# Regrouping attention heads so that two pairs share their loads

## The chip, the cores and the metric

The kernel runs on one core of a Trainium2 chip. The core has five engines that this document speaks of: PE (TensorE, matmuls and transposes through the PE array), DVE (VectorE), ACT (ScalarE), POOL (GpSimd) and SP (SyncE, which here only issues transfers). Each engine takes its instructions strictly in its own order and stops at an instruction whose semaphore has not come. The metric is the device time of one execution in microseconds (us).

## The reference

Three layers follow one another: attention with a decay, a mixture of experts with one expert per token, and a gated feed-forward layer. The change touches only the first:

```python
# q, k, v: (4, 8, 576, 64), f: (4, 8, 576)
scores = scale * np.matmul(q, k.transpose(0, 1, 3, 2))
cum = np.cumsum(np.log(np.clip(f, 0.0001, 1.0)), axis=-1)
decay = cum[:, :, :, None] - cum[:, :, None, :]
scores = np.where(causal, -1000000000.0, scores + decay)
scores = scores - np.max(scores, axis=-1, keepdims=True)
attn = np.exp(scores)
attn = attn / (np.sum(attn, axis=-1, keepdims=True) + 1e-09)
attn_out = np.matmul(attn, v)
# then x = attn_out as (4 * 576, 512) -> moe(x) -> gated layer(x)
```

In every row of scores the term of the query's own `cum` is constant and drops out of the softmax, so the kernel only needs the key's `cum` ("the sums"), the same for all queries of a head.

## The kernel before, in words

**Stages.** Attention takes the first 222.6 us of the span, then comes a short tail in which the last tokens are routed and scattered to their experts (to 240.4 us), then the experts and the gated layer (to the end). The change leaves the code of the last two alone, except for the order of three weight loads.

**Pairs.** Attention works on 16 pairs of heads, four pairs to each of the four batches; pair p of a batch is heads 2p and 2p + 1. The 576 queries of a head are cut in five chunks: chunks 0 to 3 of 128 queries, and a last one of 64. The last 64 queries of both heads of a pair are stacked, head 0 on partitions 0 to 63 and head 1 on partitions 64 to 127; this chunk is called 4. A pair goes through its chunks from 4 down to 0, and causality makes chunk c read only the keys up to its own.

**Steps of a pair.** SP loads queries and keys (`load_qk`, L344, eight transfers of 72 KB in runs of 128 bytes), V (`load_v`, L336, two of 128 KB and one of 32 KB), the sums of both heads copied to all 128 partitions, keys 0 to 511 (`load_bc`, L356, 512 KB), and for chunk 4 a second copy of the sums, all 576 keys, in which partitions 0 to 63 hold head 0 and 64 to 127 hold head 1 (`load_dec`, L363, two of 144 KB). DVE transposes queries and keys (L402). POOL spreads the last queries (`qk_z`, L446), adds the causal mask of the last 64 keys to the second copy (`dec_m`, L454), and masks the diagonal block of every chunk and head in the common copy (`bc_m`, L459, eight per pair, chunk 3 first). PE makes the scores (L469 for chunk 4, the first of a pair; L481 for the others), DVE adds the sums and takes each row's extreme in one pass (L495; L505 for chunk 4, in two halves of 288 keys over all 128 partitions), ACT takes the exponentials (L513), PE transposes the result (L528) and DVE or ACT bring it to SBUF (L541, L539), and PE multiplies by V (L581). After each batch POOL multiplies the tokens by their route and scatters them (L729, L737), in between the pairs of the next batch. `zero_rows` (L620) clears the place of the scattered tokens by one transfer of 640 KB.

**What sets the order.** The order of every engine is fixed when the kernel is built. A planner (`Plan`, L59) list-schedules about 100 tasks for each pair with assumed durations and priorities. A task's priority is its pair number plus an offset from the table `PR`; a task can only be planned when its inputs and its buffers (`NB`, L269) are there by the planner's own times. On the chip each engine keeps that order whatever the real times are. So a `dec_m` whose transfer lands later than was planned holds every mask that stands behind it on POOL, and by these masks DVE and PE.

**Buffers.** Two tiles for queries and two for keys (one pair each), three for the common copy of the sums, three for the second copy, four for V, two for scores in PSUM.

```python
o.bc = two.tile([P, 2, 512], F32, tag="bc", name="bc", bufs=NB["bc"])
nc.sync.dma_start(out=o.bc, in_=cum_d[None, h : h + 2, :512].to_broadcast([P, 2, 512]))
d = pairs[p].dec[:, 512:576]
nc.gpsimd.tensor_tensor(out=d, in0=d, in1=future, op=ALU.add)
```

Of the kernel before, what the change touches and what calls it, by code (L numbers as in the profile page):

```python
# [24 lines left out]
    ldd=-0.906,  # L25
    ldq=-2.409,
    ldk=-2.46,
    bc=-1.878,
    ldv=-1.485,
    tq=-3.414,  # L30
    tk=-2.813,
    z=-3.857,
    dc=4.332,
    sc=0.044,
    mx=-0.165,
    ex=0.003,
    tr=0.413,
    ev=0.272,
    mk=-0.849,
    rsc=2.696,  # L40
    av=0.888,
    ave=-2.088,
    tok=1.048,
    toe=-2.57,
    rt=1.92,
    rm=0.004,
    rw=2.342,
    step=0.149,
    zr=0.627,
    stick=0.371,  # L50
    w=1.575,
    ws=-0.918,
# [105 lines left out]
def moe_kernel(ctx: ExitStack, tc: tile.TileContext, q, k, v, f, wgate, w1, w2, m2g, m2v, m2o, out):  # L158
# [78 lines left out]

    sel = one.tile([P, NP, 2, W2], F32, name="sel")
# [7 lines left out]
    v_sb = pairwise("v_sb", [P, NC, 2, D], 4)  # L246
# [109 lines left out]
    def load_bc(p):  # L356
        b, hp = divmod(p, NP)
        o = pairs[p]
        o.bc = two.tile([P, 2, 512], F32, tag="bc", name="bc", bufs=NB["bc"])
        h = b * H + 2 * hp  # L360
        nc.sync.dma_start(out=o.bc, in_=cum_d[None, h : h + 2, :512].to_broadcast([P, 2, 512]))

    def load_dec(p):  # L363

        b, hp = divmod(p, NP)
        o = pairs[p]
        o.dec = two.tile([P, S], F32, tag="dec", name="dec", bufs=NB["dec"])
        h = b * H + 2 * hp
        for x in range(2):
            nc.sync.dma_start(  # L370
                out=o.dec[x * 64 : x * 64 + 64], in_=cum_d[None, h + x, :].to_broadcast([64, S])
            )

    def bc_mm(hh, x, st):

        if hh == 2:
# [4 lines left out]
        st.n = 288 if hh == 2 else 256
        st.ps = s_tile()[:, 0]

        for h, a, m in ((0, 0, 64), (1, 64, 64)) if hh == 2 else ((hh, 0, P),):
            nc.tensor.matmul(
                st.ps[a : a + m, : st.n], lhsT=ident[: B * H, h : h + 1].to_broadcast([B * H, m]),
                rhs=setup[1][:, x * st.n : x * st.n + st.n], start=True, stop=True,
            )

    def bc_ev(hh, x, st):  # L390
        o = pairs[0]
        d = o.dec if hh == 2 else o.bc[:, hh]
        nc.scalar.activation(out=d[:, x * st.n : x * st.n + st.n], in_=st.ps[:, : st.n], func=AF.Copy)
# [4 lines left out]
    def qk_t(p, i):  # L398
# [3 lines left out]
        nc.vector.transpose(out=o.t[:, i], in_=o.qk[i][:, :S])  # L402
# [1190 lines left out]
```

## Time and profile before

| | us |
|---|---|
| median of 3 runs (924.0 to 925.56) | 924.26 |
| the profiled execution | 927.53 |
| its span | 925.3 |
| attention, from the span's start | 222.6 |
| routing and scatter of the last tokens | 222.6 to 240.4 |
| experts and gated layer | 240.4 to 925.3 |

The profiled execution is 3.27 us above the median, 2.23 us of it outside the span. Over the span PE is busy 96%, DVE 63%, ACT 43% and POOL 29%. PE's share is lower and the transfers' share higher in the first quarter, where attention is.

In the rows below, a row of the stage table has the stretch, its length, and then for each engine the busy us with the number of instructions, the granted TensorE clock (1.00 is full speed), the share of the DMA engines' time that was in use, and GB/s. A row of a timeline has the start, the duration, the engine, the line, the operation, output and inputs, and in brackets the idle time just before it with what ended it. A row of the waits has the waiting engine and line, who it waited for, the total in us, how often, and the longest. A row by line and shape has the engine, operation and shape with its count, then the busy time and the mean in ns of one, then the idle time before the group with what ended it.

### The profile page before, as it was taken

How to read it: one execution, taken by the hardware profiler on the slowest of the kernel's cores; microseconds unless marked ns; L12 is line 12 of the kernel's file. 1: busy time of each engine (PE TensorE's matmuls, PEld its weight loads, DVE VectorE, ACT ScalarE, POOL GpSimd, SP SyncE). 2: the span in 40 equal slices, each digit the busy share in tenths (PEclk: the TensorE clock that was granted, in tenths of full speed). 3: DMA queues.
4: the chain of work that ended last, by engine and by line, in shares of the span. 5: the costliest groups of instructions: out<-in, count | busy, mean ns of one | idle time of the engine just before them, and what ended most of it. 6: DMA issues, size and time to landing. Idle time of an engine off the chain costs nothing. (4 is left out here: it accounts for less than half of the span.)

```text
span 925.3 us, 15341 instructions
## 1 busy us (share of the span) xinstructions
PE 892.0 (96%) x5100; PEld 729.0 (79%) x5100; DVE 585.7 (63%) x1439; ACT 399.4 (43%) x958; POOL 268.9 (29%) x369
## 2 busy tenths in 40 slices
PE   8989899997999999999999999999999999999996
PEld 4546565664799999999978888888888888888875
DVE  5656576686576677878824366565574765746754
ACT  6757677785354555555535322122221222222210
POOL 4224425263000000000214243242342433423335
PEclk9989999998999999999999999999999999999998
DMA  6897777561675667667422011020111110200013
GB/s 134 174 187 151 187 145 189 132 182 37 181 201 165 195 168 215 191 195 214 118 93 69 23 46 46 23 69 23 46 46 46 46 46 24 69 23 23 1 69 136
DMA packets 160416, 100.11 MB, mean 108 GB/s; under 512 B 98320, under 2 KB 142480, under 8 KB 160336
## 3 DMA queue, kind: packets, MB, share of 16 engines
q1 hardware_dynamic: 157424, 89.68, 37.8%
q0 software_dynamic: 2912, 9.44, 2.7%
q8 instruction: 40, 0.66, 0.3%
q14 instruction: 40, 0.33, 0.1%
HBM read 84.21 MB, written 14.88 MB: 107 GB/s over the span
## 5 line engine op out<-in xcount | busy, mean ns | idle before, releaser
L1519 PE MATMUL r<-hl,phl 128*128 128x512 f32 x594 | 146.3, 393 | 0.1
L1502 DVE TENSOR_TENSOR sg<-v,sg 128x512 f32<-128x512 f32 (+1 forms) x60 | 38.2, 637 | 154.6 <-PE v L1492 145.8
L1492 PE MATMUL v<-yh,hl 128*128 128x512 f32 (+1 forms) x440 | 134.8, 372 | 0.0
L1492 PE MATMUL g<-yh,hl 128*128 128x512 f32 (+1 forms) x440 | 134.3, 370 | 0.0
L1347 POOL TENSOR_TENSOR cs<-ca,cs 128x512 f32<-128x512 f32 x36 | 47.2, 1312 | 290.1 <-DVE cs L1343 290.1
L1519 PEld LDWEIGHTS r<-hl,phl 128*128 128x128 f32 x594 | 110.6, 188 | 25.0 <-DVE acc L1524 0.5
L1524 DVE TENSOR_TENSOR acc<-r,acc 128x512 f32<-128x512 f32 x198 | 127.1, 683 | 3.9 <-PE r L1519 3.7
L1076 PE MATMUL h<-xhl,hl 128*128 128x320 f32 (+6 forms) x768 | 121.4, 307 | 0.5 <-DVE hl L780 0.5
L1095 PE MATMUL y<-hh,hl 128*128 128x320 f32 (+6 forms) x768 | 120.2, 305 | 0.0
L1507 POOL TENSOR_TENSOR phl<-sg,phl 128x512 fp32r<-128x512 f32 (+1 forms) x55 | 68.6, 1246 | 164.9 <-ACT phl L1504 152.7
L1076 PEld LDWEIGHTS h<-xhl,hl 128*128 128x128 f32 x768 | 112.5, 188 | 1.2 <-DVE hl L780 0.7
L1095 PEld LDWEIGHTS y<-hh,hl 128*128 128x128 f32 x768 | 112.5, 188 | 0.2 <-DVE hh L1081 0.2
L1504 ACT ACTIVATE phl<-sg 128x512 fp32r<-128x512 f32 (+1 forms) x60 | 35.4, 591 | 167.2 <-DVE sg L1502 167.2
L513 ACT ACTIVATE u<-u,mn 128x576 f32<-128x576 f32 (+2 forms) x144 | 83.8, 584 | 39.8 <-DVE mn L495 27.3
L1492 PEld LDWEIGHTS g<-yh,hl 128*128 128x128 f32 x440 | 80.3, 188 | 15.3
L1492 PEld LDWEIGHTS v<-yh,hl 128*128 128x128 f32 x440 | 80.3, 188 | 15.1
L1501 ACT ACTIVATE sg<-g 128x512 f32<-128x512 f32 (+1 forms) x60 | 33.4, 556 | 136.4 <-PE g L1492 135.0
L495 DVE CUSTOM_DVE_ANT_0 u<-s,bc 128x512 f32<-128x512 f32 (+3 forms) x128 | 60.2, 481 | 44.0 <-PE s L481 23.9
L780 DVE TENSOR_TENSOR hl<-raw,hl 128x512 fp32r<-128x512 f32 x128 | 85.0, 708 | 3.7 <-ACT hl L775 2.4
L1492 PE MATMUL v<-yl,hl 128*128 128x512 f32 (+1 forms) x220 | 81.2, 369 | 0.0
L1492 PE MATMUL g<-yl,hl 128*128 128x512 f32 (+1 forms) x220 | 81.1, 368 | 0.0
L775 ACT ACTIVATE hl<-raw 128x512 fp32r<-128x512 f32 x128 | 72.6, 621 | 0.0
(206 smaller groups left out, 1265.0 us busy)
## 6 DMA issues: line engine op xcount, KB each, us to landing
raw<-in_moe_w_dram SPq DMA_DIRECT2D x128, 128.0 KB, 3.0
raw<-in_moe_w_dram SPq DMA_DIRECT2D x32, 512.0 KB, 4.0
bc<-cum_d SPq DMA_DIRECT2D x15, 512.0 KB, 4.8
raw<-in_moe_w_gate_dram SPq DMA_DIRECT2D x12, 512.0 KB, 3.7
raw<-in_moe_w_val_dram SPq DMA_DIRECT2D x12, 512.0 KB, 3.7
raw<-in_moe_w_out_dram SPq DMA_DIRECT2D x12, 512.0 KB, 3.5
qk<-in_k_dram SPq DMA_DIRECT2D x60, 72.0 KB, 4.3
qk<-in_q_dram SPq DMA_DIRECT2D x60, 72.0 KB, 2.8
```

What stands on the lines that cost most here:

```text
L495: nc.vector.tensor_tensor_reduce(out=st.U[:, :W], in0=st.ps[:, at : at + W], in1=o.bc[:, hh, :W], op0=ALU.add, op1=ALU.min, scale=-0.125, ...
L513: nc.scalar.activation(out=st.U[:, :W], in_=st.U[:, :W], func=AF.Exp, bias=o.mn[:, x : x + 1], scale=-1.0, accum_out=o.sm[:, u : u + 1],)
L775: nc.scalar.activation(out=hls[e, qi][part][:, 0, j], in_=raws[e, qi][part][:, j], func=AF.Copy)
L780: nc.vector.tensor_tensor(out=t[:, 1, j], in0=raws[e, qi][part][:, j], in1=t[:, 0, j].bitcast(F32), op=ALU.subtract)
L1076: nc.tensor.matmul(ps[:, :n], lhsT=w[:, a, c, f0 : f0 + P], rhs=xhl[e][:, b, c, :n], start=m == 0, stop=m == 3 * KC - 1)
L1095: nc.tensor.matmul(ys[e][c][:, : win(e)], lhsT=w[:, a, fc % 2, c * P : (c + 1) * P], rhs=t[:, b], start=fc == 0 and m == 0, stop=fc == NF ...
L1347: nc.gpsimd.tensor_tensor(out=s.bitcast(F32), in0=a.bitcast(F32), in1=s.bitcast(F32), op=ALU.add)
L1492: nc.tensor.matmul(pgv[fc, ti][y][:, :n], lhsT=w[:, a, y, c, :], rhs=(yh, yl)[b][:, c, t0 : t0 + n], start=m == 0, stop=m == 3 * KC - 1,)
L1502: nc.vector.tensor_tensor(out=sg[:, :n], in0=pv[:, :n], in1=sg[:, :n], op=ALU.mult)
L1507: en.tensor_tensor(out=t[:, 1, :n], in0=sg[:, :n], in1=t[:, 0, :n].bitcast(F32), op=ALU.subtract)
L1519: nc.tensor.matmul(ps, lhsT=t[:, a, x : x + P], rhs=w[:, b, :DM], start=m == 0, stop=m == 2)
L1524: nc.vector.tensor_tensor(out=o, in0=ps, in1=o, op=ALU.add)
```

## The change

Pair p of a batch is now heads p and p + 4. The pairs' numbers keep their order; only the index of the head in each load, and the place of the result in the output, follow. Since two neighbouring pairs then are heads (p, p + 1) and (p + 4, p + 5), one transfer can hold two pairs: queries of two pairs come by four transfers of 144 KB, keys too, and the sums of two pairs by one of 1,152 KB, all 576 keys. Pair 1 is loaded alone, then [2, 3], [4, 5], to [14, 15]. `load_dec` and its tile go. `dec_m` adds its mask to keys 512 to 575 of the common copy, for both heads (128x2x64), and chunk 4 is reduced in two instructions of 64 partitions and 576 keys, one for each head, in place of two of 128 partitions and 288 keys. The masks L459 of a pair's common copy wait for these two, since they write where chunk 4 reads. V's last 64 rows come once for a whole batch (`load_v4`, 128 KB) and not once for each pair (32 KB). The tiles hold two pairs: two for queries, two for keys, two for the sums. `zero_rows` moves up, right behind the queries of pair 1. The table `PR` has new numbers.

```diff
-        o.qk[i] = pre.tile([P, WQ], F32, tag=f"qk{i}", name=f"qk{i}", bufs=NB[f"qk{i}"])
+    def load_qk(g, i):
+        b, hp = divmod(g[0], NP)
+        n = len(g)
+        t = pre.tile([P, GS * S], F32, tag=f"qk{i}", name=f"qk{i}", bufs=2)
+        src = (q, k)[i][b].rearrange("(s h) (t c) d -> s c h t d", s=2, c=32)
         for hh in range(2):
             for dh in range(2):
                 a = hh * 64 + dh * 32
                 nc.sync.dma_start(
-                    out=o.qk[i][a : a + 32, :S].rearrange("p (t d) -> p t d", d=32),
-                    in_=(q, k)[i][b, 2 * hp + hh].rearrange("(t c) d -> c t d", c=32)[:, :, dh * 32 : dh * 32 + 32],
+                    out=t[a : a + 32, : n * S].rearrange("p (h t d) -> p h t d", h=n, d=32),
+                    in_=src[hh, :, hp : hp + n, :, dh * 32 : dh * 32 + 32],
                 )
-    def load_dec(p):
-        for x in range(2):
-            nc.sync.dma_start(
-                out=o.dec[x * 64 : x * 64 + 64], in_=cum_d[None, h + x, :].to_broadcast([64, S])
-            )
+    def bc_tile():
+        return two.tile([P, 2, GS, S], F32, tag="bc", name="bc", bufs=2)
+
+    def load_bc(g):
+        b, hp = divmod(g[0], NP)
+        n = len(g)
+        t = bc_tile()
+        src = cum_d.rearrange("(b s h) j -> b s h j", s=2, h=NP)[b, :, hp : hp + n]
+        nc.sync.dma_start(out=t[:, :, :n], in_=src[None].to_broadcast([P, 2, n, S]))
+        for x, p in enumerate(g):
+            pairs[p].bc = t[:, :, x]
...
-        d = pairs[p].dec[:, 512:576]
-        nc.gpsimd.tensor_tensor(out=d, in0=d, in1=future, op=ALU.add)
+        d = pairs[p].bc[:, :, 512:576]
+        nc.gpsimd.tensor_tensor(out=d, in0=d, in1=future[:, None, :].to_broadcast([P, 2, 64]), op=ALU.add)
...
-        j = slice(x * 288, x * 288 + 288)
+        r = slice(x * 64, x * 64 + 64)
         nc.vector.tensor_tensor_reduce(
-            out=st.U[:, j], in0=st.ps[:, x, :288], in1=o.dec[:, j], op0=ALU.add, op1=ALU.min,
-            scale=-0.125, scalar=3.0e38 if x == 0 else o.mn[:, 8:9], accum_out=o.mn[:, 8 + x : 9 + x],
+            out=st.U[r].rearrange("p (y j) -> p y j", y=2), in0=st.ps[r, :, :288],
+            in1=o.bc[r, x].rearrange("p (y j) -> p y j", y=2), op0=ALU.add, op1=ALU.min,
+            scale=-0.125, scalar=3.0e38, accum_out=o.mn[r, 8:9],
         )
...
-                add("pool", 260, kk + PR["mk"], partial(bc_m, p, ic, hh), [lb] + [mxs[hh, c] for c in range(ic + 1, 4)])
+                add("pool", 260, kk + PR["mk"], partial(bc_m, p, ic, hh), [lb] + [mxs[hh, c] for c in range(ic + 1, 5)])
...
-    dc=4.332,
+    dc=3.712,
-    mk=-0.849,
+    mk=-5.0,
```

On POOL this is the order before, from `dec_m` of pair 2 on. `dec` is the second copy of the sums, `bc` the common copy, and `qz` in the fifth row the spread last queries of pair 4; the second row's six masks are chunk 3 of pair 3 and chunks 2 and 1 of pair 2.

```order
L454 TENSOR_TENSOR dec<-dec,future 128x64
L459 AFFINE_SELECT bc<-bc 128x128 x6
L454 TENSOR_TENSOR dec<-dec,future 128x64
L459 AFFINE_SELECT bc<-bc 128x128 x3
L446 TENSOR_TENSOR qz_164<-own,qkt 128x128
L459 AFFINE_SELECT bc<-bc 128x128 x2
L454 TENSOR_TENSOR dec<-dec,future 128x64
L459 AFFINE_SELECT bc<-bc 128x128 x6
```

These are `dec_m` of pairs 2, 3 and 4; the three masks behind pair 3's are chunk 3 of pair 4 (two) around the first of pair 2's chunk 0, and pair 4's stands between the two heads of pair 3's chunk 2. After the change the same stretch of POOL reads as follows (L451 is `dec_m`, L456 the masks, L443 `qk_z`).

```order
L451 TENSOR_TENSOR bc<-bc,future 128x2x64 x2
L456 AFFINE_SELECT bc<-bc 128x128 x7
L443 TENSOR_TENSOR qz_166<-own,qkt 128x128
L456 AFFINE_SELECT bc<-bc 128x128 x5
L451 TENSOR_TENSOR bc<-bc,future 128x2x64 x2
L456 AFFINE_SELECT bc<-bc 128x128 x3
L443 TENSOR_TENSOR qz_167<-own,qkt 128x128
L456 AFFINE_SELECT bc<-bc 128x128 x7
L451 TENSOR_TENSOR bc<-bc,future 128x2x64 x2
```

`dec_m` now comes for two pairs at once: pairs 2 and 3, then pairs 4 and 5 ahead of chunk 1 of pair 3, then pairs 6 and 7 ahead of chunk 0 of pair 4. The seven masks behind the first two are chunks 3, 2 and 1 of pair 2 and one head of its chunk 0. No mask of a later pair stands ahead of a mask of an earlier one any more.

On SP this is the order before, from the loads of pair 2 to the sums of pair 3.

```order
L351 DMA qk_320<-in_k_dram 32x18x32 x4
L351 DMA qk_352<-in_q_dram 32x18x32 x4
L370 DMA dec<-cum_d 64x576 x2
L361 DMA bc<-cum_d 128x2x512
L339 DMA v_sb_156<-in_v_dram 128x4x64 x2
L342 DMA v_sb_156<-in_v_dram 64x2x64
L351 DMA qk_453<-in_k_dram 32x18x32 x4
L351 DMA qk_479<-in_q_dram 32x18x32 x4
L620 DMA xs<-warm 640x1x256
L370 DMA dec<-cum_d 64x576 x2
L361 DMA bc<-cum_d 128x2x512
```

The two rows of `dec` are pairs 1 and 2, the two of `bc` pairs 2 and 3. After the change SP issues this from the loads of pair 1 to the sums of pairs 4 and 5 (L360 queries and keys, L375 sums, L343 and L349 V, L619 the zeros).

```order
L360 DMA qk_252<-in_q_dram 32x18x32 x4
L619 DMA xs<-warm 640x1x256
L349 DMA v_158<-in_v_dram 64x8x64
L343 DMA v_sb_154<-in_v_dram 128x4x64 x2
L375 DMA bc<-cum_d 128x2x576
L360 DMA qk_307<-in_k_dram 32x36x32 x4
L360 DMA qk_336<-in_q_dram 32x36x32 x4
L343 DMA v_sb_155<-in_v_dram 128x4x64 x2
L343 DMA v_sb_156<-in_v_dram 128x4x64 x2
L375 DMA bc<-cum_d 128x2x1152
L360 DMA qk_425<-in_k_dram 32x36x32 x4
L360 DMA qk_463<-in_q_dram 32x36x32 x4
```

Then follow V of pair 3 and of the next batch's last rows, the queries of pairs 6 and 7, and the sums of pairs 4 and 5. The zeros and V have moved ahead of the sums of pair 1, and queries and keys of two pairs ahead of the sums of the first of them.

## Rows read from the trace of the kernel before

**Rows 1.** Stage table, attention in four stretches of four pairs.

```profile
11.70:65.00 53.30, 46.03 (x286) 27.41 (x285) 29.37 (x110) 32.97 (x101) 12.60 (x43) 0.94 0.90 178
65.00:117.00 52.00, 47.59 (x340) 30.96 (x338) 33.58 (x137) 37.67 (x119) 21.81 (x52) 0.97 0.74 163
117.00:167.00 50.00, 47.70 (x342) 31.07 (x338) 33.47 (x137) 37.75 (x119) 21.99 (x52) 0.97 0.72 162
167.00:222.60 55.60, 54.04 (x396) 35.64 (x395) 39.04 (x161) 44.00 (x139) 20.10 (x43) 1.00 0.48 125
```

**Rows 2.** Timeline of PE, first scores of pairs 3, 4, 12 and 13.

```profile
46.03 1.24 PE L469 MATMUL s<-qkt,qz 128*128 128x288 f32 x4
...
65.00 1.24 PE L469 MATMUL s<-qkt,qz 128*128 128x288 f32 x4
...
167.02 1.24 PE L469 MATMUL s<-qkt,qz 128*128 128x288 f32 x4
...
178.51 1.24 PE L469 MATMUL s<-qkt,qz 128*128 128x288 f32 x4
```

**Rows 3.** Timeline of PE, its longest waits within pairs 3 to 12.

```profile
52.87 2.08 PE L481 MATMUL s<-qkt 64*128 64x512 f32 x4 [4.45 <-DVE mn L495]
...
80.08 1.13 PE L481 MATMUL s<-qkt 64*128 64x512 f32 x4 [1.20 <-DVE mn L495]
...
106.58 0.41 PE L528 MATMUL pt<-ident,u 128*128 128x128 f32 x2 [2.71 <-ACT u L513]
...
156.45 0.41 PE L528 MATMUL pt<-ident,u 128*128 128x128 f32 x2 [1.83 <-ACT u L513]
```

**Rows 4.** Stage table, 4 us stretches at or behind such waits.

```profile
52.00:56.00 4.00, 3.13 (x10) 1.30 (x12) 2.78 (x13) 2.87 (x10) 0.72 (x3) 0.53 1.00 134
108.00:112.00 4.00, 4.00 (x26) 1.75 (x22) 2.12 (x9) 2.17 (x6) 0.58 (x2) 0.71 0.70 167
160.00:164.00 4.00, 4.00 (x29) 2.48 (x26) 0.87 (x3) 1.65 (x4) 1.06 (x4) 0.81 0.84 160
```

**Rows 5.** Waits of attention: POOL for transfers, DVE for POOL.

```profile
POOL dec L454 <- DMA dec<-cum_d: 33.2, 13, 6.2
POOL bc L459 <- DMA bc<-cum_d: 33.1, 12, 6.1
DVE u L495 <- POOL bc L459: 19.9, 22, 2.8
```

**Rows 6.** Timeline of POOL, 46 to 52 us.

```profile
49.72 0.32 POOL L454 TENSOR_TENSOR dec<-dec,future 128x64 f32<-128x64 f32 x1 [6.24 <-DMA dec<-cum_d]
51.03 0.78 POOL L459 TENSOR_SCALAR_AFFINE_SELECT bc<-bc 128x128 f32<-128x128 f32 x3 [0.99 <-DMA bc<-cum_d]
```

**Rows 7.** Timeline of DVE around 47 us, then 173 to 175 us.

```profile
47.50 0.78 DVE L402 STREAM_TRANSPOSE qkt<-qk 128x576 f32<-128x576 f32 x1 [2.62 <-DMA qk<-in_q_dram]
...
173.55 0.49 DVE L541 COPY p<-pt 128x128 f32<-128x128 f32 x2 [1.38 <-PE pt L528]
174.63 0.56 DVE L495 CUSTOM_DVE_ANT_0 u<-s,bc 128x384 f32<-128x384 f32 x1 [0.59 <-POOL bc L459]
```

**Rows 8.** Stage table, a stretch mostly of queries and keys, one of sums.

```profile
40.00:44.00 4.00, 3.93 (x33) 2.60 (x29) 2.47 (x11) 3.98 (x14) 1.61 (x6) 1.00 0.83 97
148.00:152.00 4.00, 4.00 (x35) 2.70 (x33) 1.55 (x7) 3.60 (x11) 2.84 (x6) 1.00 1.17 322
```

**Rows 9.** Timeline of SP's own queue, issues of keys for pairs 1 and 3.

```profile
8.53 2.21 SPq L351 DMA_DIRECT2D qk<-in_k_dram  x4
...
25.20 4.51 SPq L351 DMA_DIRECT2D qk<-in_k_dram  x4
```

**Rows 10.** Attention by line and shape: the passes of DVE over scores.

```profile
L495 DVE CUSTOM_DVE_ANT_0 u<-s,bc 128x512 f32<-128x512 f32 x32 | 21.7, 679 | 0.9 <-PE s L481 0.9
...
L495 DVE CUSTOM_DVE_ANT_0 u<-s,bc 128x384 f32<-128x384 f32 x32 | 16.9, 555 | 15.2 <-PE s L481 9.6 <-POOL bc L459 5.6
...
L505 DVE CUSTOM_DVE_ANT_0 u<-s,dec,mn 128x288 f32<-128x288 f32 x16 | 8.1, 508 | 0.4
...
L505 DVE CUSTOM_DVE_ANT_0 u<-s,dec 128x288 f32<-128x288 f32 x16 | 7.3, 456 | 7.5 <-ACT xl L603 2.7 <-ACT u L513 2.1 <-PE s L469 2.0
```

More of the change, by code (lines that the diff above doesn't have):

```diff
@@ L24 @@
 PR = dict(
[L25 to L32, printed above, removed]
-    dc=4.332,
[L34 to L38, printed above, removed]
-    mk=-0.849,
[L40 to L52, printed above, removed]
+    lv4=-1.428,
+    ldq=-3.063,
+    ldk=-3.075,
+    bc=-2.083,
+    ldv=-1.295,
+    tq=-7.302,
+    tk=-6.629,
+    z=-3.444,
+    dc=3.712,
+    sc=-0.047,
+    mx=-0.263,
+    ex=3.31,
+    tr=0.172,
+    ev=0.213,
+    mk=-5.0,
+    rsc=1.628,
+    av=0.805,
+    ave=-7.286,
+    tok=1.112,
+    toe=-0.862,
+    rt=-1.883,
+    rm=4.39,
+    rw=-3.344,
+    step=0.099,
+    zr=-1.476,
+    stick=0.346,
+    w=3.229,
+    ws=-3.248,
     ev_eng="aaaaadadddd",
@@ L257, in moe_kernel @@
         nc.gpsimd.memset(own[x * 64 : x * 64 + 64, x], 1.0)
-    for i in range(4):
-        nc.gpsimd.memset(v_sb[i][64:, NC - 1], 0.0)
     for i in range(2):
+        nc.gpsimd.memset(v4[i][64:], 0.0)
         nc.gpsimd.memset(p3[i][64:], 0.0)
@@ L268, in moe_kernel @@
     NKEEP = 48
-    NB = dict(qk0=2, qk1=2, bc=3, qkt=2, dec=3, u=6, pt=2, s=2, t=2, o=2, v=4, x=2, xo=1, z=2)
+    NB = dict(qk0=4, qk1=4, bc=4, qkt=2, u=6, pt=2, s=2, t=2, o=2, v=4, x=2, xo=1, z=2)
     plan = Plan(NB)
-    WQ = NC * 2 * D
+    GS = 2
+    LOADS = [[1]] + [[p, p + 1] for p in range(2, NPR, 2)]
     class Pair:
@@ new lines, in load_qk @@
+                    in_=src[hh, :, hp : hp + n, :, dh * 32 : dh * 32 + 32],
+                )
+        for x, p in enumerate(g):
+            pairs[p].qk[i] = t[:, x * S : x * S + S]
+    def bc_tile():
[6 more added lines that the diff above has]
+        nc.sync.dma_start(out=t[:, :, :n], in_=src[None].to_broadcast([P, 2, n, S]))
+        for x, p in enumerate(g):
+            pairs[p].bc = t[:, :, x]
@@ L390, in bc_ev @@
+    def bc_mm(hh, x, st):
+        if hh == x == 0:
+            pairs[0].bc = bc_tile()[:, :, 0]
+        st.ps = s_tile()[:, 0]
+        nc.tensor.matmul(
+            st.ps[:, :288], lhsT=ident[: B * H, hh * NP : hh * NP + 1].to_broadcast([B * H, P]),
+            rhs=setup[1][:, x * 288 : x * 288 + 288], start=True, stop=True,
+        )
     def bc_ev(hh, x, st):
-        o = pairs[0]
-        d = o.dec if hh == 2 else o.bc[:, hh]
-        nc.scalar.activation(out=d[:, x * st.n : x * st.n + st.n], in_=st.ps[:, : st.n], func=AF.Copy)
+        nc.scalar.activation(out=pairs[0].bc[:, hh, x * 288 : x * 288 + 288], in_=st.ps[:, :288], func=AF.Copy)
@@ L401, in qk_t @@
             qk_new(p)
-        nc.vector.transpose(out=o.t[:, i], in_=o.qk[i][:, :S])
+        nc.vector.transpose(out=o.t[:, i], in_=o.qk[i])
     def first_load(i, x):
@@ L829, in chain, with loads, half @@
         return ids
+    lds = {}
+    v4s = {}
+    def loads(p):
+        g = next((g for g in LOADS if p in g), None)
+        if g is None or g[0] in lds:
+            return lds.get(g and g[0])
+        n = len(g)
+        p = g[0]
+        lds[p] = [
+            add("sp", 2160, p + PR["ldq"], partial(load_qk, g, 0), acq=["qk0"] * 2, data=1870 * n),
+            add("sp", 2160, p + PR["ldk"], partial(load_qk, g, 1), acq=["qk1"] * 2, data=1870 * n),
+            add("sp", 600, p + PR["bc"], partial(load_bc, g), [fs], acq=["bc"] * 2, data=1700 * n),
+        ]
+        return lds[p]
+    def half(p, name):
+        g = next((g for g in LOADS if p in g), [p])
+        return [name] * (2 if len(g) == 1 else 1)
+    tts = {}
+    mx0 = {}
     sl = add("sp", 1300, -5, sel_load, data=450)
@@ L836, in moe_kernel @@
             xdone.setdefault((b, x), [])
-        ldv = add("sp", 1775, p + PR["ldv"], partial(load_v, p), [avs[p - 4]] if p > 3 else [], acq=["v"], data=1240)
+        ldv = add("sp", 1100, p + PR["ldv"], partial(load_v, p), [avs[p - 4]] if p > 3 else [], acq=["v"], data=1100)
+        if hp == 0:
+            v4s[b] = add(
+                "sp", 550, p + PR["lv4"], partial(load_v4, b), [avs[p - NP - 1]] if b > 1 else [], data=600,
+            )
         if p == 0:
@@ L850, in moe_kernel @@
             lb = None
[L851 to L852 removed]
+            for hh in range(2):
                 for x in range(2):
                     st = St()
[L855 to L856 removed]
+                    m = add("pe", 605, -50, partial(bc_mm, hh, x, st), [fn], acq=["s"] + (["bc"] * 2 if hh == x == 0 else []))
                     lb = add("act", c_act(288), -50, partial(bc_ev, hh, x, st), [m, lb], rel=["s"])
[L858 to L868 removed]
+        else:
+            ld = loads(p)
+            lb = ld[2]
+            tt = [add("dve", 690, p + PR["tq"], partial(qk_t, p, 0), [ld[0], *tts.get(p - 1, [])], acq=["qkt"], rel=half(p, "qk0"))]
+            tt.append(add("dve", 690, p + PR["tk"], partial(qk_t, p, 1), [ld[1], tt[0]], rel=half(p, "qk1")))
+            tts[p] = tt[1:]
         z = add("pool", 420, p + PR["z"], partial(qk_z, p), tt[:1] if p else tt[4:5], acq=["z"])
[L870 removed]
+        dc = add("pool", 280, p + PR["dc"], partial(dec_m, p), [lb])
         ex = {}
@@ L930, in moe_kernel @@
                     "dve", c_dve(W), kk + PR["mx"] + 0.001 * hh, mx_fn,
-                    [pm, mk[hh], first_mx, mxs.get((0, ic))] + ([mxs[hh, 1]] if ic == 0 else []),
-                    acq=["u"], rel=(["s"] if ic != 1 and hh else []) + (["bc"] if ic == 0 and hh else []),
+                    [pm, mk[hh], first_mx, mxs.get((0, ic))] + ([mxs[hh, 1]] if ic == 0 else []) + ([mx0.get(p - 1)] if ic == 0 else []),
+                    acq=["u"], rel=(["s"] if ic != 1 and hh else []) + (half(p, "bc") if ic == 0 and hh else []),
                 )
+                mx0[p] = mx
                 ex[hh, ic] = e = add("act", 280 + 0.833 * W, kk + PR["ex"] + 0.001 * hh, partial(sc_exp, p, u, W, st), [mx])
```

79 lines of the change are left out of this document (21 added, 58 removed).

## The prediction

> **What bounds the kernel now.** I read the stage table first, then PE's timeline in attention, then the waits, and last POOL's and the transfers' timelines around each stop. The stage table [rows 1] is to show where time can be won: attention's four stretches of four pairs take 53.3, 52.0, 50.0 and 55.6 us, 210.9 together. All else is code that the change leaves alone; only three weight loads change places behind attention, and I cost that at nothing, since the tail's waits are for tokens.
>
> PE's timeline gives the floor. Pair 12 runs from 167.02 to 178.51 us [rows 2], 11.49 us, at clock 1.00 and without a stop; four such pairs are 46.0 us. In the first stretch PE stops for 4.45 us, in the second for 1.20 and 2.71, in the third for 1.83 [rows 3], always for a score pass of DVE or what hangs on one. Each stop costs more than itself: at and behind it the granted clock reads 0.53, 0.71 and 0.81 [rows 4], so that behind the last two another (1 - 0.71) x 4 = 1.2 us and (1 - 0.81) x 4 = 0.8 us go.
>
> Who ends these stops? In the waits [rows 5] POOL waits 33.2 us at `dec_m` and 33.1 us at the masks for sums to land, and DVE waits 19.9 us for POOL's masks. The timeline of POOL [rows 6] shows one case: `dec_m` of pair 3 stands 6.24 us until 49.72 and the masks behind it 0.99 us more, until pair 4's sums land at 51.03. Among those is pair 2's chunk 0, due long before; DVE and PE wait for it until 52.87 [rows 3]. So POOL's fixed order puts a later pair's transfer ahead of the current pair's mask. The first stretch is bound by transfers as well: their share is 0.90 [rows 1], and DVE waits 2.62 us for queries until 47.50 [rows 7].
>
> **The change, part by part.** Transfers first. The second copy goes (15 pairs x 288 KB), the common copy grows from 512 to 576 KB a pair. A stretch mostly of queries and keys moves 97 GB/s at share 0.83, or 117 at full share; one mostly of sums 322 at 1.17, or 275 [rows 8]. With these prices queries and keys (590 kB a pair) take 5.0 us, the old sums 1.9 + 1.1, the new 2.1, a saving of 0.9 a pair. V's 262 kB I estimate at 1.3 us, between 0.95 and 2.2 by the two prices; the zeros at 2.4 and V's last rows at 0.7.
>
> Does such a sum hold? Run over the old order from SP's first key transfer at 8.53 [rows 9] it lands pair 4's queries at 44.8; they landed at 47.50 [rows 7]. It is up to 3 us early, so a landing below may be up to 8% later.
>
> The new order from 8.5: pair 1's queries and keys 13.5; zeros 2.4, V 0.7 + 1.3, sums 2.1: 20.0; queries and keys of pairs 2 and 3 (10.1) 30.1; V of two pairs and their sums (2.6 + 4.3) 37.0; queries and keys of 4 and 5 47.1; V and last rows 2.0, queries of 6 and 7 5.0: 54.1; sums of 4 and 5 58.4 (62.4 with the 8%); V and keys of 6 and 7 64.7.
>
> Now the work. Pair 2's two `dec_m` wait until 37.0. Each is 0.32 us today [rows 6] for 64 columns; 128 take 0.32 to 0.64, I take 0.45. So pair 2's chunk 4 reaches DVE at 37.9. In pair 12 it does so 1.7 us behind the pair's first scores, and 9.8 us remain to the next pair: 47.7. Pair 4's queries land at 47.1, and their transposes (0.78) stand on DVE in front of pair 2's last passes, so pair 3 starts at about 48, against 46.03 [rows 2]. Here the change loses 2 us. In exchange the 4.45 us stop goes, because nothing of pair 4 stands ahead of pair 3's chunk 3. What is late next is `dec_m` of pairs 4 and 5, ahead of pair 3's chunk 1: POOL can go on at 58.4 + 0.9 + 0.3 = 59.6, where by pair 12's pace (9.9 us behind the first scores) the mask is due at 57.9. Queued behind on POOL are all of pair 3's remaining masks, and on them DVE and PE. Pair 4 starts at 48 + 11.5 + 1.7 = 61.2, against 65.00: **-3.8 us**. The same landing 3.7 us earlier would give 57.5; 4 us later 65.2.
>
> Second stretch: the stops of 1.20 and 2.71 and 1.2 of clock go, -5.1. Sums of pairs 6 and 7 wait for their buffer, free when pair 3's chunk 0 is through, 0.9 us behind pair 4's first scores; but the queue still has work to 64.7 then, and V (1.3) and the queries of pairs 8 and 9 (5.0) stand ahead of them, so they land at 75.3. `dec_m` of both and a mask (1.2) make that 76.5, where chunk 0 of pair 4 is due 12.0 us into the pair, at 73.2: +3.3. From then on two pairs need 10.1 + 4.3 + 2.6 + 0.7 = 17.7 us of transfers against 23.0 us of PE, so the backlog goes; the next group's sums land some 0.3 us late (between 1 early and 1 late). Sum: 52.0 - 5.1 + 3.3 + 0.3 = 50.5, **-1.5 us**. Third: 1.83 + 0.8 go, two groups come at 0.3: **-2.0 us**. Fourth: no stop to remove, one group at 0.3 and 0.1 of DVE: **+0.4 us**.
>
> DVE's part: chunk 4 took 456 + 508 ns in two passes [rows 10]. A pass over 576 columns of half the partitions is not in the trace. The rows of 384 and 512 columns rise by 124 ns for 128, so 576 cost 0.74, and two 1.48: +0.52 us a pair. Below, if half the partitions took half the time, 0.74 in all: -0.22. The rows show full width at every size, so I take +0.52. It hides where DVE idles behind it: 1.38 and 0.59 us ahead of pair 12's chunk 2 [rows 7]. Where the next batch's routing fills DVE, in four pairs, 0 to 0.5 us each; I took 0.1 in the fourth stretch, the rest is in the range. The Trainium skill ("VectorE: DVE Perf Modes", "Two Vector instructions with no wait between them") has a rule against this edit: an instruction that starts in another group of 32 partitions than its forerunner is held until that has finished. By it the pass on partitions 64 to 127 and the one behind it would each lose the overlap of neighbours, an estimate of 0.2 us a pair beside the 0.52; no run shows it yet, and the same idle time takes it.
>
> Masks now wait for both chunk 4 passes. Behind them on POOL stand the pair's other masks and, in a batch's second pair, the routed tokens. DVE itself takes chunk 4 first, so the wait costs no more than 0.3 us, the mask ahead of chunk 3, inside the landings' error. The removed transfers and the shared V rows free SP's queue, which nothing but a transfer waits for.
>
> Sum: -3.8 - 1.5 - 2.0 + 0.4 = **-6.9 us**. The profiled execution would go from 927.53 to 920.6; the median of the runs, 3.27 us lower, from 924.26 to **917.4**.
>
> **Rivals.** *All stops go.* Transfers of twice the size keep the transfer engines fuller: SP stood 4.51 us at the keys of pair 3 [rows 9] where pair 1's took 2.21, so it was waiting for places in flight and not for work. If sums of 4 and 5 land 3.7 us earlier, pair 4 starts at 57.5 (-7.5), and -5.1 and -2.6 follow: -15.2, 909 us. Against it: the share is 0.90 to 1.00 in the first stretch already [rows 1, 4]. The Trainium skill ("DMA: Bandwidth & Descriptors", "Rules for kernel authors") stands on its side: it wants many small transfers made into one large one, and 1 MiB or more in each. By that the sums gain and the 128-byte runs of queries and keys need not.
>
> *Nothing comes of it.* Landings are 8% late: pair 4 starts at 65.2, the later stops are replaced by 3.3 + 0.6 + 0.6 us and more of the kind: 924 us.
>
> *Slower.* The sums of two pairs as a unit come late in each group. `dec_m` of both pairs stands ahead of the current pair's masks at six places, pairs [4, 5] to [14, 15], and the buffer for the sums, only two tiles, frees no earlier than the last chunk of the pair two groups back. Each such stop is then like the one worked out for pairs 4 and 5 with late transfers, 3.7 us, plus 0.8 of clock [rows 4]: 4.5 x 6 = 27, less 15.2: +11.8, 936 us. It decides from 2.5 us a group on. For it: the buffer's free time leaves 11 us for queries of the next group and sums, which need 5.0 + 4.3. Against: the share falls to 0.74 and 0.72 behind 65 us [rows 1], with 0.9 us a pair less to move. That the change doesn't shrink the transfers can't be: the second copy is gone.
>
> **How the numbers follow.** Forecast 0.50, all stops go 0.17, nothing 0.13, slower 0.20. No change means within 0.2%, 1.8 us, about what a measurement can tell: faster takes the first two, 0.67; same 0.13; slower 0.20. The forecast's own range, from landings 2 us either way and the DVE bounds, is 912 to 922. The range leaves out half of the 909 case and most of the 936 case: 908 to 928.
>
> **What would show it.** Right: the rows of POOL waiting for the second copy are gone, and its waits for sums drop from 66.3 us to under 35; pair 4's first scores at 59 to 63; pair 12's at 152 to 162; chunk 4's passes at 0.7 to 0.8 us, and PE not waiting for them. Wrong: pair 4 starts at 65 or later (transfers slower than priced), stops of over 2.5 us at POOL's `dec_m` in each of the later groups (slower), or a last stretch of over 58 us (DVE's passes are not covered).

## The result and the profile after

The changed kernel takes 912.45 us (median of 4 runs, 912.36 to 914.51) against 924.25 us: ratio 0.9875, interval 0.9858 to 0.9892. It is 11.8 us faster, where 6.9 were forecast; the forecast of 917.4 had the sign and the place right and the size too small. Between the two profiled executions the difference is larger, 927.53 to 912.42, 15.1 us, because that of before lies 3.3 us above its median and that of after on it. The stretches below come from these two executions alone.

The stage table after, for the stretches from the first scores of pairs 0, 4, 8 and 12 to those of the next, and last from pair 12 to the first expert matmul. Columns as before: stretch, length, busy us of PE, PE's weight loads, DVE, ACT and POOL with counts, granted clock, transfer share, GB/s.

```profile
10.90:57.80 46.90, 42.53 (x292) 26.49 (x292) 31.57 (x110) 33.56 (x103) 13.01 (x41) 1.00 1.04 189
57.80:106.60 48.80, 46.26 (x340) 30.36 (x339) 36.32 (x139) 37.70 (x119) 23.34 (x52) 1.00 0.77 155
106.60:153.10 46.50, 45.93 (x341) 30.47 (x340) 35.98 (x137) 37.38 (x120) 22.88 (x51) 1.00 0.73 154
153.10:226.30 73.20, 65.40 (x443) 40.19 (x443) 51.36 (x217) 46.18 (x148) 28.34 (x54) 0.95 0.41 119
```

Against [rows 1] the first three lost 6.4, 3.2 and 3.5 us, and their clock reads 1.00 in place of 0.94 to 0.97. The last is the sum of two stretches of before (55.6 + 17.8 = 73.4) and has not moved. Pair 0 starts 0.8 us earlier (10.9 for 11.7). The three gains, this start and the last stretch make 14.1 of the 15.7 us between the two spans; the other 1.6 us lie behind the first expert matmul, in code that the change leaves alone. DVE is busier in each of the first three although they are shorter, by 2.2 to 2.7 us, and chunk 4 accounts for 2.2 of it.

PE's timeline after, the first scores of pairs 3, 4, 8 and 12, and the one stop of over 1.3 us that is left among the pairs:

```profile
45.62 1.14 PE L466 MATMUL s<-qkt,qz 128*128 128x288 f32 x4
57.79 1.14 PE L466 MATMUL s<-qkt,qz 128*128 128x288 f32 x4
106.62 1.14 PE L466 MATMUL s<-qkt,qz 128*128 128x288 f32 x4
153.07 1.14 PE L466 MATMUL s<-qkt,qz 128*128 128x288 f32 x4
72.52 0.41 PE L526 MATMUL pt<-ident,u 128*128 128x128 f32 x2 [1.68 <-ACT u L511]
```

Pair 4 starts at 57.79 and not at 65.00 [rows 2]; of the four stops of [rows 3], 10.2 us of idle PE, one of 1.68 us is left in their place. The waits of attention that answer to [rows 5] (total, times, longest):

```profile
POOL bc L451 <- DMA bc<-cum_d: 14.0, 7, 4.2
DVE u L492 <- POOL bc L456: 9.3, 16, 2.2
```

POOL's 66.3 us for sums have become 14.0, all at `dec_m` (L451). Its timeline shows when the sums of pairs 2 and 3, 4 and 5, 6 and 7 land, and DVE's what waits for a mask behind two of them:

```profile
36.33 0.87 POOL L451 TENSOR_TENSOR bc<-bc,future 128x128 f32<-128x128 f32 x2 [2.34 <-DMA bc<-cum_d]
55.26 0.87 POOL L451 TENSOR_TENSOR bc<-bc,future 128x128 f32<-128x128 f32 x2 [2.96 <-DMA bc<-cum_d]
70.46 0.86 POOL L451 TENSOR_TENSOR bc<-bc,future 128x128 f32<-128x128 f32 x2 [4.16 <-DMA bc<-cum_d]
```

```profile
56.41 0.42 DVE L492 CUSTOM_DVE_ANT_0 u<-s,bc 128x256 f32<-128x256 f32 x1 [2.17 <-POOL bc L456]
71.60 0.29 DVE L492 CUSTOM_DVE_ANT_0 u<-s,bc 128x128 f32<-128x128 f32 x1 [1.85 <-POOL bc L456]
```

These are the two waits that the forecast described, at pair 3's chunk 1 and pair 4's chunk 0. Its landings were 37.0, 58.4 and 75.3. Last, the pass over chunk 4, by line and shape, answers to [rows 10]:

```profile
L503 DVE CUSTOM_DVE_ANT_0 u<-s,bc 64x576 f32<-64x576 f32 x32 | 24.1, 754 | 5.8 <-POOL bc L451 2.5 <-PE s L466 1.4 <-issue 0.7
```

754 ns twice against 456 + 508: +0.54 us a pair, where +0.52 was estimated.

### The profile page after: what moved, and what is told of

It is laid out like the page before. It is cut to its first block, busy times and chain, and to the rows that moved or that the text cites. A ratio compares the mean times of both kernels' runs of the same rounds, so it can differ in the third digit from the quotient of the medians.

```text
span 909.6 us, 15167 instructions
## 1 busy us (share of the span) xinstructions
PE 881.5 (97%) x5089; PEld 724.5 (80%) x5092; DVE 596.0 (66%) x1439; ACT 398.5 (44%) x956; POOL 273.7 (30%) x367
## 4 chain that ended last, share of the span: by engine, by line
PE 47%; issue 2%; POOL 1%; DVE 0%; POOLq 0%; ACT 0%; DVEq 0%
PE g L1512 16%; PE v L1512 16%; PE r L1539 15%; POOL out_dram L1547 1%; DVE acc L1544 0%; POOLq L1608 0%; DVE sg L1522 0%; DVE phl L1527 0%; ACT phl L1524 0%; POOLq L1547 0%; DVEq L1522 0%
## 5 line engine op out<-in xcount | busy, mean ns | idle before, releaser
L1367 POOL TENSOR_TENSOR cs<-ca,cs 128x512 f32<-128x512 f32 x36 | 47.2, 1312 | 290.4 <-DVE cs L1363 290.4
L1512 PEld LDWEIGHTS v<-yh,hl 128*128 128x128 f32 x440 | 80.3, 188 | 15.1
```

The costliest lines, as they stand in the source:

```text
L1367: nc.gpsimd.tensor_tensor(out=s.bitcast(F32), in0=a.bitcast(F32), in1=s.bitcast(F32), op=ALU.add)
L1512: nc.tensor.matmul(pgv[fc, ti][y][:, :n], lhsT=w[:, a, y, c, :], rhs=(yh, yl)[b][:, c, t0 : t0 + n], start=m == 0, stop=m == 3 * KC - 1,)
```

## The experiments

Behind the first row the kernels come in three groups of four, each group on one chip beside runs of the kernel before on the same chip. There the kernel before scattered more, from 922.0 to 930.5 us, so ratios to it are what compares across groups.

| kernel | median us | before us | ratio | interval |
|---|---|---|---|---|
| changed, first | 912.45 | 924.25 | 0.9875 | 0.9858 to 0.9892 |
| POOL's order alone | 912.0 | 925.77 | 0.9844 | 0.9816 to 0.9872 |
| split transfers | 924.95 | 925.77 | 0.9992 | 0.9973 to 1.0011 |
| second copy loaded | 920.6 | 925.77 | 0.9945 | 0.9927 to 0.9963 |
| `dec_m` in time | 916.1 | 925.77 | 0.9886 | 0.9857 to 0.9914 |
| changed, second | 915.08 | 925.49 | 0.9873 | 0.9843 to 0.9903 |
| V first | 914.13 | 925.49 | 0.9869 | 0.9841 to 0.9897 |
| chunk 4 passes twice | 928.94 | 925.49 | 1.0035 | 1.0015 to 1.0056 |
| one pair, in time | 914.96 | 925.49 | 0.9878 | 0.9851 to 0.9906 |
| POOL's order alone, again | 911.03 | 927.59 | 0.9832 | 0.9803 to 0.9861 |
| changed, third | 914.27 | 927.59 | 0.9856 | 0.9828 to 0.9884 |
| order and chunk 4 by head | 916.71 | 927.59 | 0.9884 | 0.9856 to 0.9912 |
| split, `dec_m` in time | 918.46 | 927.59 | 0.9908 | 0.9875 to 0.9941 |

**POOL's order alone.** In the kernel before, one dependency more:

```diff
-        dc = add("pool", 280, p + PR["dc"], partial(dec_m, p), [ldc])
+        dc = add("pool", 280, p + PR["dc"], partial(dec_m, p), [ldc] + mlast[-1:])
...
-                add("pool", 260, kk + PR["mk"], partial(bc_m, p, ic, hh), [lb] + [mxs[hh, c] for c in range(ic + 1, 4)])
+                add("pool", 260, kk + PR["mk"], partial(bc_m, p, ic, hh), [lb, *mprev] + [mxs[hh, c] for c in range(ic + 1, 4)])
...
+            if ic == 0:
+                mlast.append(mk[1])
```

(`mprev` is the last mask of the pair before.)

> The kernel before with one edit: dec_m and the masks of a pair may only come behind the last mask of the pair before, so nothing of a later pair stands ahead of a current mask on POOL; transfers, bytes and chunk 4 as before. Theory A (POOL's order held DVE and PE, and the order is most of the gain): the stops of 80, 106 and 156 us go with their clock loss, about -7, and part of the 4.45 us stop: 913 to 918. Theory B (fewer bytes land sooner, the order matters little): 921 to 925.

It gave 13.8 us, more than theory A's upper end. This kernel is called the mended kernel below. POOL's timeline around 46 us, where [rows 6] show 6.24 us of waiting:

```profile
46.74 0.79 POOL L459 TENSOR_SCALAR_AFFINE_SELECT bc<-bc 128x128 f32<-128x128 f32 x3
47.65 0.32 POOL L454 TENSOR_TENSOR dec<-dec,future 128x64 f32<-128x64 f32 x1
50.21 0.29 POOL L459 TENSOR_SCALAR_AFFINE_SELECT bc<-bc 128x128 f32<-128x128 f32 x1 [2.24 <-DVE mn L495]
```

`dec_m` of pair 3 now comes behind pair 2's masks and waits for nothing, though the transfers are those of before. The masks wait for DVE's earlier passes over the same sums, as they must. Over attention POOL's waits at `dec_m` for transfers fall from 33.2 us to 2.5, and the 33.1 us of the masks are gone. Pair 4 starts 8.2 us earlier than in [rows 2]:

```profile
56.81 1.24 PE L469 MATMUL s<-qkt,qz 128*128 128x288 f32 x4
```

The planner runs anew with the added dependency. SP's transfers of attention keep their order to the last one, and DVE, ACT and PE keep theirs up to 92 us of before; behind that a few of their instructions change places. So the 8.2 us up to pair 4 come from POOL's order alone; in the rest (14.8 us by the start of pair 12) those few moves may have a share. Neither fewer bytes nor larger transfers are needed to win back what the stops cost.

**Split transfers, second copy, `dec_m` in time.** All three start from the changed kernel.

```diff
+                for x in range(n):
+                    nc.sync.dma_start(
+                        out=t[a : a + 32, x * S : x * S + S].rearrange("p (t d) -> p t d", d=32),
+                        in_=src[hh, :, hp + x, :, dh * 32 : dh * 32 + 32],
+                    )
```

(the same for the sums)

> The changed kernel with each transfer of two pairs cut into two of one pair, at the same place of the queue; all orders the same. Theory C (larger transfers fill the engines better, which made the landings some us earlier than priced): sums of pairs 4 and 5 land 3 us later or more, 915 to 918. Theory D (the size of a transfer is not what counts): within 1 us of 912.4, or up to 1 us less, since the first pair's half lands sooner.

It lost the whole gain. POOL's and SP's timelines of the split kernel:

```profile
58.31 0.46 POOL L453 TENSOR_TENSOR bc<-bc,future 128x128 f32<-128x128 f32 x1 [2.95 <-DMA bc<-cum_d]
60.87 0.45 POOL L453 TENSOR_TENSOR bc<-bc,future 128x128 f32<-128x128 f32 x1 [2.11 <-DMA bc<-cum_d]
77.71 0.45 POOL L453 TENSOR_TENSOR bc<-bc,future 128x128 f32<-128x128 f32 x1 [6.22 <-DMA bc<-cum_d]
79.58 0.45 POOL L453 TENSOR_TENSOR bc<-bc,future 128x128 f32<-128x128 f32 x1 [1.42 <-DMA bc<-cum_d]
```

```profile
15.27 8.98 SPq L361 DMA_DIRECT2D qk<-in_k_dram  x8
```

The sums of pair 1 land alike in both, first the changed kernel, then the split one:

```profile
21.05 0.45 POOL L451 TENSOR_TENSOR bc<-bc,future 128x128 f32<-128x128 f32 x1 [1.89 <-DMA bc<-cum_d]
```

```profile
21.22 0.45 POOL L453 TENSOR_TENSOR bc<-bc,future 128x128 f32<-128x128 f32 x1 [1.55 <-DMA bc<-cum_d]
```

From there to the sums of pair 7 it is 49.4 us with large transfers and 58.4 with small ones, for the same bytes in the same order: 18% more. The DMA engines' share over these stretches is 1.06 and 0.84. Whether the sums or the queries and keys lose more by the cut, no run separates. SP spends 8.98 us on issuing keys of pairs 2 and 3, where the changed kernel's row is this:

```profile
15.15 6.42 SPq L360 DMA_DIRECT2D qk<-in_k_dram  x4
```

Each late landing holds POOL at `dec_m`, and PE stops:

```profile
81.22 0.66 PE L528 MATMUL pt<-ident,u 128*128 128x128 f32 x2 [5.18 <-ACT u L513]
```

> The changed kernel that also loads a second copy of the sums again (496 of its 576 columns, two transfers of 124 KB for each pair, behind the sums), which nothing reads. Theory B (bytes): 254 kB a pair at 275 GB/s is 0.9 us; three pairs' stand ahead of the sums of pairs 4 and 5, five ahead of those of 6 and 7: pair 4 starts 2.8 us later, pair 6 some 2 us more: 915 to 918. Theory A (order): the later stretches have room for it, and only what the first two stretches lose shows: 912.5 to 914.5.

```diff
+            spare = two.tile([P, 496], F32, tag="spare", name="spare", bufs=2)
+            for y in range(2):
+                nc.sync.dma_start(
+                    out=spare[y * 64 : y * 64 + 64],
+                    in_=cum_d[None, b * H + y * NP + hp + x, :496].to_broadcast([64, 496]),
+                )
```

It lost 0.0070 of ratio, 6.5 us, more than theory B's. In POOL's timeline the sums of 4 and 5, and of 6 and 7, land 4.5 and 6.8 us later than in the changed kernel:

```profile
59.73 0.88 POOL L457 TENSOR_TENSOR bc<-bc,future 128x128 f32<-128x128 f32 x2 [3.38 <-DMA bc<-cum_d]
77.22 0.86 POOL L457 TENSOR_TENSOR bc<-bc,future 128x128 f32<-128x128 f32 x2 [6.44 <-DMA bc<-cum_d]
```

So in the changed kernel bytes do count. That they count because of where `dec_m` stands is argued, not tested: the mended kernel loads a second copy as well, and its `dec_m` wait only 2.5 us. No run has both the spare copy and `dec_m` in time.

> The changed kernel with dec_m of each pair held back behind the last mask of the pair before, so that the wait for the next group's sums no longer stands ahead of current masks. If the two stops that are left (DVE waits of 2.17 us at 56.4 and 1.85 us at 71.6 for POOL) are the price of dec_m in pairs: 908 to 910.5. If what is left is bound by landings anyhow, the wait comes back at chunk 4 of pairs 4 and 6: 911.5 to 913.

The edit is the first line of that for POOL's order. A miss: the two waits of DVE are gone, but pairs 4, 8 and 12 start at 58.78, 106.69 and 154.39, not clearly earlier than in the three executions of the changed kernel (57.79 to 58.95, 106.62 to 109.73, 153.07 to 156.19), and the ratio is within its interval. The planner has moved more than `dec_m` here: behind some 84 us, PE, DVE and ACT have other orders than in the changed kernel. So the run shows that this edit wins nothing that can be measured; what the two waits cost by themselves stays open.

**Split, `dec_m` in time.** Both edits together.

> The changed kernel with its transfers cut into one pair each and dec_m behind the last mask of the pair before. If the smaller transfers cost 12 us only because dec_m of two pairs stood ahead of current masks when the sums landed late: the loss goes, 913 to 918. If the smaller transfers are slow by themselves, beyond POOL's order: 921 to 926.

From 0.9992 to 0.9908, intervals apart: most of what splitting cost, some 7.8 us, came back by moving `dec_m`, with the same new orders of the other engines as in the run before. With large transfers the same move changes nothing that can be measured. Large transfers, then, are worth 11 us in one order, and about 2 in the other, where the intervals overlap.

**V first.** One term of the landings was read from the wrong row: I began at 8.5 us, but in the changed order V of pair 0 comes behind pair 1's keys and queries, the queue begins at 6.8, and the sum counts that V all the same.

```diff
-        ldv = add("sp", 1100, p + PR["ldv"], partial(load_v, p), ...
+        ldv = add("sp", 1100, p + PR["ldv"] - (2 if p == 0 else 0), partial(load_v, p), ...
```

> The changed kernel with V of pair 0 loaded where it was before, ahead of pair 1's keys and queries. The forecast's sum of landings began at 8.5 us, but the changed queue begins at 6.8, since V moved. If landings bind the first stretch from its start (theory B, and the explanation of 1.75 of the 3.1 us by which the sums of pairs 4 and 5 came early): pair 4 starts 1.5 to 1.8 us later, +1.5 to +2.5 in all with the stop at pair 5. If the early start is taken up by waits that end with other things: +0 to +0.7.

The sums of pairs 4 and 5 land at 55.62 us, pair 4 starts at 57.78, and the ratio does not move. But the run can't tell what the early start was worth. In SP's timelines, first of the changed kernel, then of this one, the queue begins at the same time, only with V:

```profile
6.78 2.11 SPq L360 DMA_DIRECT2D qk<-in_k_dram  x4
```

```profile
6.79 1.03 SPq L343 DMA_DIRECT2D v_sb<-in_v_dram  x2
7.87 2.12 SPq L360 DMA_DIRECT2D qk<-in_k_dram  x4
```

The same bytes go ahead of the sums of pairs 4 and 5 in both, so their landing had no reason to move. What the run shows is that the order of V and pair 1's keys doesn't matter.

**Chunk 4 passes twice.** In `sc_max4`, `for _ in range(2):` around the instruction.

> The changed kernel with each of the two passes of DVE over chunk 4 issued twice (same operands, same result): +1.66 us of DVE a pair, 26.6 in all. If DVE has room behind chunk 4 as forecast (the 0.52 us that the change added were free): idle of about 2 us a pair takes most of it, +2 to +8. If DVE is on the path of the changed kernel, all of it shows: +20 to +27.

0.0162 of ratio, 15 us of the 26.6 added: a little over half shows. The cover is smaller than the forecast took it to be, and the next kernel measures the real edit.

**Order and chunk 4 by head.** In the mended kernel the two passes of the change, on the second copy:

```diff
-        j = slice(x * 288, x * 288 + 288)
+        r = slice(x * 64, x * 64 + 64)
...
-            out=st.U[:, j], in0=st.ps[:, x, :288], in1=o.dec[:, j], op0=ALU.add, op1=ALU.min,
-            scale=-0.125, scalar=3.0e38 if x == 0 else o.mn[:, 8:9], accum_out=o.mn[:, 8 + x : 9 + x],
+            out=st.U[r].rearrange("p (y j) -> p y j", y=2), in0=st.ps[r, :, :288],
+            in1=o.dec[r].rearrange("p (y j) -> p y j", y=2), op0=ALU.add, op1=ALU.min,
+            scale=-0.125, scalar=3.0e38, accum_out=o.mn[r, 8:9],
```

> The kernel before with POOL's order mended and chunk 4 reduced as in the change (two passes of 64 partitions and 576 columns, reading the second copy as before): +0.55 us of DVE a pair, 8.8 in all, and nothing else. If the forecast's cover holds: within 1 us of the mended kernel. If DVE is near its limit once the stops are gone (the doubled passes showed more than half of what they added): +3 to +6.

+5.7 us, of 8.8 added; the six runs of each do not overlap (909.38 to 914.39 and 915.32 to 917.89), and the orders of all engines but for the two passes are the same through attention. The stretch from 100 to 150 us, first of the mended kernel, then of this one:

```profile
100.00:150.00 50.00, 49.41 (x365) 32.81 (x364) 34.24 (x143) 39.58 (x125) 22.25 (x52) 1.00 0.87 184
```

```profile
100.00:150.00 50.00, 47.45 (x346) 31.21 (x348) 37.08 (x144) 37.94 (x119) 21.69 (x50) 1.00 0.83 175
```

DVE is busy 2.8 us more and PE 2.0 us less. In the timeline of PE stops appear that the mended kernel does not have, at a pass of chunk 4, at a copy on DVE, and at the transposes of chunk 4's exponentials, which ACT (first row of the second block) could only start when the second pass had ended, at 138.73. Its bracket names a copy on DVE, but that had ended at 137.93.

```profile
29.01 0.92 PE L481 MATMUL s<-qkt 64*128 64x384 f32 x4 [1.05 <-DVE mn L505]
...
127.78 0.18 PE L677 MATMUL pt<-onehot,tri 128*128 128x40 bf16 x1 [0.86 <-DVE p L542]
```

```profile
138.82 0.78 ACT L514 ACTIVATE u<-u,mn 128x576 f32<-128x576 f32 x1 [3.73 <-DVE p L542]
139.74 0.65 PE L529 MATMUL pt<-ident,u 128*128 128x128 f32 x4 [1.07 <-issue]
```

Stops like the last two of PE come once in each of three batches.

**One pair, in time.** The changed kernel with `GS = 1`, every group one pair, three tiles of queries and keys and four of sums, and `dec_m` in time.

> The changed kernel with one pair in each transfer (tiles: three of queries and keys, four of sums) and dec_m behind the last mask of the pair before: one copy of the sums, no unit of two pairs, nothing of a later pair ahead of a mask. If the order of POOL and the fewer bytes are the gain and the size of a transfer is not: 906 to 911. If grouping itself is worth what the split transfers lost (12 us): 918 to 926.

A miss for the first theory, by 4 us as measured and by 2 at this ratio of 924.25, but grouping is not worth 11: at 0.9878 it is level with the changed kernel. With `dec_m` in time, one copy of the sums pair by pair is neither better nor worse than the changed kernel's by two; here too the planner gave the other engines new orders.

**Again, beside each other.** The mended kernel and the changed one on one chip:

> The kernel before with only POOL's order mended, once more, beside the changed kernel on one chip: 0.984 to 0.987 of before. If it is no slower than the changed kernel here too, the larger transfers, the one copy of the sums and the fewer bytes add nothing to the order.

> The changed kernel beside the mended one on the same chip: 0.986 to 0.989 of before, as twice so far.

911.03 (909.38 to 914.39) and 914.27 (911.68 to 914.95). The mended kernel was ahead by 3.2 us here and by 0.0031 of ratio earlier, though the intervals overlap: it is at least level. With these medians of one chip, a way from the kernel before to the changed one has three steps: from 927.59 POOL's order takes 16.6 to 911.03, chunk 4 by head gives back 5.7 to 916.71, and all the rest (larger transfers, one copy, fewer bytes, the new table `PR`) takes 2.4 to 914.27. Another way would divide the sum otherwise, since the changed kernel's own order of POOL, with `dec_m` in pairs, is not the mended one.

## Why the prediction came out as it did

**The mechanism was right.** POOL's order put a later pair's sums ahead of a current mask, and these stops went. That is shown by the kernel with that one dependency more. Of the signs named, POOL's waits for sums (14.0 us, under 35), the start of pair 12 (153.07) and the length of chunk 4's passes (754 ns) came as stated; pair 4 started at 57.79, ahead of the 59 to 63 given.

**First stretch, -3.8, measured -6.4.** The path was the forecast one, and two terms on it were too long. Pair 3 was to start at 48 and started at 45.62, which is 9.3 us behind the landing of the sums of pairs 2 and 3 at 36.33; the forecast had 11 us behind 37.0. DVE reached pair 2's chunk 4 at 36.82, behind one `dec_m` and not two, and pair 3 came 8.8 us behind that, not 10.1; why the pair's rest was so short no run shows. The wait for the sums of pairs 4 and 5 was to cost 1.7 us, and pair 4 started only 12.2 us behind pair 3, 0.7 over the 11.5 of an undisturbed pair: the sums landed at 55.26 and not at 58.4. So 2.4 of the 3.4 us by which pair 4 came ahead of 61.2 are pair 3's. In two more executions of the changed kernel (its second and third row in the table) pair 3 starts at 47.09 and 47.22, again 9.3 us behind the landing, and pair 4 at 58.95 and 58.53, so the wait costs 0.4 us and nothing; the stretch is 47.2 and 47.1 us.

The landings were priced too late from the sums of pair 1 on: 55.3 us were worked out to those of pairs 6 and 7 (20.0 to 75.3), and large transfers took 49.4, small ones 58.4. The price of queries and keys came from a stretch of 72 KB transfers [rows 8] and was used for transfers of 144 KB. That transfers of twice the size land sooner was the first rival's argument, with SP's 4.51 us [rows 9] in its favour; I gave it 0.17, and a little over half of what it had beyond the forecast came (4.9 of 8.3 us). The rule of the Trainium skill that stood beside it ("DMA: Bandwidth & Descriptors", "Rules for kernel authors": many small transfers into one large) agrees with the trace here: 49.4 against 58.4 us. The queue's early start, which I had missed, was used up at once: pair 1's sums landed at 21.05 where 20.0 was worked out, so the first part of the sum was too cheap by more than the start gave.

Two sums in the forecast don't hold. The check over the old order comes to about 43.3 us by its own prices and not 44.8, so a landing could have been 12% late, not 8%. And a landing 3.7 us earlier could not by itself bring pair 4 to 57.5, since with pair 3 at 48 the work alone lasts to 59.5; pair 4 came to 57.79 because pair 3 started earlier.

**Second and third stretch, -1.5 and -2.0, measured -3.2 and -3.5.** The stop at pairs 6 and 7 was forecast as 3.3 us and was 1.68 on PE, their sums landing at 70.46 and not at 75.3. Here one execution misleads. In the two others the same stop is this:

```profile
74.61 0.41 PE L526 MATMUL pt<-ident,u 128*128 128x128 f32 x2 [3.00 <-ACT u L511]
```

```profile
73.47 0.41 PE L526 MATMUL pt<-ident,u 128*128 128x128 f32 x2 [2.28 <-ACT u L511]
```

Their second stretch takes 50.8 and 50.4 us, -1.2 and -1.6, about as forecast. After that the landings are hardly late: 0.3 us for each group was too much, and the third stretch is 46.5, 46.5 and 47.1 us in the three, 0.5 to 1.1 above four times pair 12's 11.49 [rows 2].

**Fourth stretch, +0.4, measured -0.2.** Right within what one execution can tell; the measured figure takes in the tail.

**DVE's part.** The duration was right (754 for 0.74), the cover wrong. I read 1.38 and 0.59 us of idle time in pair 12 [rows 7] as room for 0.5 us. But that idle time lies behind chunk 3, and the exponentials of chunk 4 wait for its extreme at once. In the waits of the mended kernel and of the one with chunk 4 by head, ACT's for that extreme are these:

```profile
ACT u L513 <- DVE mn L505: 14.0, 11, 4.9
```

```profile
ACT u L514 <- DVE mn L505: 22.6, 13, 5.3
```

8.6 us more (10.5 against the mended kernel's other execution), about the 8.8 added, and 5.7 of it reached the end. The result of the changed kernel hides this, since the larger gain of the order stands against it. If the passes cost the changed kernel as much, it is in part luck that the total came no further from the forecast: a cost left out stood against landings priced too late. On the held instruction the timeline of DVE in that kernel agrees with the rule of the Trainium skill ("VectorE: DVE Perf Modes", "Two Vector instructions with no wait between them"):

```profile
137.65 0.28 DVE L542 COPY p<-pt 128x128 f32<-128x128 f32 x1
137.96 0.76 DVE L505 CUSTOM_DVE_ANT_0 u<-s,dec 64x576 f32<-64x576 f32 x1
138.65 0.08 DVE L505 DVE_READ_ACCUMULATOR2_ANT mn<- 64x1 f32 x1
138.76 0.69 DVE L495 CUSTOM_DVE_ANT_0 u<-s,bc 128x512 f32<-128x512 f32 x1
```

The pass on partitions 64 to 127 starts 0.03 us after the copy has ended, and the pass of 128 partitions 0.03 us after the accumulator's read; that read itself starts 0.07 us before the end of its pass. So the two held starts cost about 0.1 us each, the 0.2 us a pair that was estimated.

**The slower rival.** Its mechanism is real, and the split kernel is it: 14 waits at `dec_m`, 29.8 us, PE stopped for 5.18 us, and the gain gone. It did not come here since the larger transfers land the unit of two pairs nearly in time. Even so the split kernel is level with the kernel before (0.9992), not 11.8 us slower as the rival had it. What kept the rival away was the term of the landings, which I had put too late.

**What I didn't see.** I worked out each part against the path and never asked which of them was needed. One dependency in the planner gives all of it, by the medians 3 us more.

## What to carry to other kernels

When an engine with a fixed order waits for a transfer, look first at what stands behind the waiting instruction, and whether it needs that transfer: moving the instruction may give what a rework of the transfers gives, and it makes the kernel less sensitive to when they land (splitting the transfers cost 11 us in one order and 2 in the other). A transfer's price, read at one size, may not hold at twice the size. Idle time on an engine covers an edit only if it lies between the edit and the next instruction that someone waits for.

## What the runs showed of the hardware

Splitting transfers of 144 KB in runs of 128 bytes into 72 KB, and those of 1,152 KB into 576 KB, made the same queue 18% longer (58.4 for 49.4 us), and SP took 8.98 us in place of 6.42 to issue the same keys. A score pass of DVE over 64 partitions and 576 columns took 754 ns, in line with 128 partitions (555 for 384, 679 for 512; 741 by that slope): half the partitions saved nothing. POOL's addition took 320 ns for 64 columns [rows 6] and 456 for 128 (the mean of 16 after the change, where two take 0.87 us).
